# First MLP boundary: w2 products ahead of their row dots, one accumulator tile, last dots behind the norm

## The chip, the cores and the metric

One core of one Trainium2 chip runs the whole program in one launch. The metric is the device time of that core in microseconds (us), lower is better. The core has five engines that run side by side, each working through its own queue in order: PE (TensorE, matmuls and transposes), DVE (VectorE), ACT (ScalarE), POOL (GpSimd) and SP (SyncE, which here only issues DMA transfers). Sixteen DMA engines move data between HBM and the on-chip memory. An instruction waits in its queue until the semaphores that it names have been raised by the work that it depends on, and everything behind it in the same queue waits with it.

## What is computed

A decode step for one token through four layers, forward and backward: attention A, MLP B, attention A, MLP B, with the same weights and the same K and V caches in both attention layers. The loss gradient is given, and all gradients of inputs, weights and caches are outputs.

```python
def _A_ref(x, k_cache, v_cache, wq, wo):          # x: 1 x 1 x 1024, caches: 4 x 65536 x 128
    q = (x @ wq).reshape(B, Sq, Hq, Dh).transpose(0, 2, 1, 3)   # 32 heads of 128
    k = jnp.repeat(k_cache, rep, axis=1)
    v = jnp.repeat(v_cache, rep, axis=1)
    p = _softmax(einsum("bhqd,bhkd->bhqk", q, k) * Dh ** -0.5)
    o = einsum("bhqk,bhkd->bhqd", p, v)
    return o.transpose(0, 2, 1, 3).reshape(B, Sq, Hq * Dh) @ wo

def _B_ref(x, w1, b1, w2, b2):                    # w1: 1024 x 3584, w2: 3584 x 1024
    h = einsum("bsd,df->bsf", x, w1) + b1
    r = where(h > 0, h, 0)
    return einsum("bsf,fd->bsd", r * r, w2) + b2

x = A_x
x = x + _A_ref(_layernorm(x), ...)                # layer 1
x = x + _B_ref(_layernorm(x), ...)                # layer 2
x = x + _A_ref(_layernorm(x), ...)                # layer 3
x = x + _B_ref(_layernorm(x), ...)                # layer 4
```

## The kernel before

The kernel streams the caches through on-chip memory four times: attention layer 1, attention layer 3, the backward pass of layer 3, and the backward pass of layer 1, which also writes the gradients of both caches. Between them stand the MLP layers. The large gradients are written in the last pass.

**Memory.** The large on-chip areas are seven pairs (`pair0` to `pair12`) of two halves with 1 MB each, the tile `eT3`, whose four halves are used as areas until layer 3 needs them, and `small`, a tile of eight blocks of 128 x 1024 for transposed blocks and one broadcast vector. A `Ring` hands out the least recently used half (`slab`, L278: one transfer into one half) or pair (`Stream.fetch`, L301: one transfer of 2 MB). A transfer may start once whatever last used its area is done; SP issues transfers in order, so one that waits holds back those behind it.

**Products.** `mv_slab` (L405) multiplies one 128-row block of a weight matrix with a column of the activations: eight matmuls with a single column for 1024 columns of weights, accumulated into one PSUM tile over all blocks.

**Row dots.** The gradient of the hidden activations of layer 4 needs the product of every row of w2 with `grad_out`. Both are known as soon as w2 passes by, so the kernel does this work in layer 2, while w2 is on the chip: `RowDots.block` takes the 28 row blocks of w2 one by one and picks for each the cheapest of four ways by a running estimate of the load of DVE, ACT and PE:

- A: one fused multiply and sum on DVE (L463);
- B: a multiply on DVE (`dot_va`, L427), then a sum on ACT (L428);
- C: eight transposes on PE (L474) into a PSUM tile, a copy to `small` on DVE (L477), eight dots on PE (L482) into an accumulator tile of one column, and a copy of that column to `y` on DVE (L483);
- D: as C, with the copy on ACT (L479).

The multiplies of A and B write over the block in place, so they wait for the product that reads the same block.

**The first boundary.** After attention layer 1: the output projection (two slabs of Wo), the norm, eight slabs of w1, the hidden activations (`mlp_hidden`), then seven slabs of w2 with four row blocks each. For each row block the program has its product and then its row dot. `mlp_close` (L755, then L385) adds the bias and the residual; `new_layer` holds the norm of layer 3 (`ln_fwd`, L348 to L365); `q_first` loads two slabs of Wq and computes the query of the first head group; then `attn_fwd` begins. Its first 40 of 256 items (an item is eight blocks of 128 rows of K) need no load and no transposes, since layer 1 kept their transposed K in ten areas: they are scores only (L686), with a copy on ACT (L691) and a maximum on DVE (L692). In the meantime `q_rest` loads the remaining three groups' Wq in eight slabs of 768 KB and adds their products between the items; `q_at=(2, 3)` puts the first one at item 2 and each next one three items later. From item 40 on K is loaded in pairs (2 MB), transposed on PE (L667) and copied (L152 on ACT, L155 on DVE).

**Order.** The program is written once in one sequence, and the framework's scheduler then sets each engine's queue by its own estimates; the queues can differ from the order of the text. SP's order of transfers around this boundary is: seven w2 slabs, two Wq slabs for `q_first`, eight for `q_rest`, then K, and V when it is needed.

Past the first items of layer 3 the diff touches nothing; `dg4`, the result of the row dots, is first used in layer 4.

Of the kernel before, what the change touches and what calls it, by code (L numbers as in the profile page):

```python
# [11 lines left out]
ALU = mybir.AluOpType  # L12
AX = mybir.AxisListType
PSUM = bass.MemoryType.PSUM
P = 128
# [3 lines left out]
def kernel(  # L19
# [24 lines left out]
    nc = tc.nc  # L44
    NOSYNC = mybir.DependencyInfo(mybir.DependencyClass.NoSync, mybir.DependencyReason.DATA)
    D = A_x.shape[-1]
# [8 lines left out]
    DC, FC = D // P, F // P  # L55
    C = SK // P
# [32 lines left out]
    def ps_tr():  # L89
        return PS["pool"].tile([P, 8, P], BF, name="ps_tr", tag="tr", bufs=2 if PS["pass4"] else 3)  # L90
# [7 lines left out]
    def ps_acc(shape):  # L98
        return PS["pool"].tile(shape, F32, name="ps_acc", tag="acc", bufs=1)
# [17 lines left out]
    def ps_bg(shape, dtype=F32):  # L117
        return ps_small("bg", shape, dtype)
# [4 lines left out]
    ident_b = const.tile([P, P], BF, name="ident_b")  # L123
# [33 lines left out]
    def add_load(act=0.0, dve=0.0):  # L157
        load["act"] += act
        load["dve"] += dve
# [10 lines left out]
    for i in range(0, 14, 2):  # L170
        t = main.tile([P, 2 * SLOT], BF, name="pair%d" % i)
# [6 lines left out]
    small = main.tile([P, SMALL], BF, name="small")  # L178
# [4 lines left out]
    def part(ap, i, n):  # L183
        return ap[:, i * n:(i + 1) * n]
# [91 lines left out]
    def slab(src, a, n):  # L276
        v = ring.slot()[:, 0:a * n].rearrange("p (a n) -> p a n", n=n)
        nc.sync.dma_start(out=v, in_=src)  # L278
        return v
# [109 lines left out]
    def w_rows(W, r0, nk, c0, ncol):  # L389

        return W[r0:r0 + nk * P, c0:c0 + ncol].rearrange("(k p) n -> p k n", p=P)

    def slabs(W, r0, KC, c0, ncol):

        per = max(1, min(KC, SLOT // ncol))
        for k0 in range(0, KC, per):
            kn = min(per, KC - k0)
            v = slab(w_rows(W, r0 + k0 * P, kn, c0, ncol), kn, ncol)
            for kk in range(kn):
                yield k0 + kk, v[:, kk, :]  # L400

    def mv_slab(out, view, kc, KC, ncol, xcol):
        nb_ = ncol // P
        for nb in range(nb_):
            nc.tensor.matmul(out[:, nb:nb + 1], lhsT=view[:, nb * P:(nb + 1) * P], rhs=xcol,  # L405
                             start=(kc == 0 and nb == 0), stop=(kc == KC - 1 and nb == nb_ - 1), skip_group_check=True)
# [18 lines left out]
    def dot_va(view, vbc, ycol, n):  # L425

        nc.vector.tensor_tensor(out=view, in0=view, in1=vbc, op=ALU.mult)  # L427
        nc.scalar.activation(out=view, in_=view, func=ACTF.Copy, accum_out=ycol)  # L428
        add_load(act=0.39 + n * 0.00086, dve=0.14 + n * 0.00053)

    class RowDots:
# [14 lines left out]
        def block(self, kc, view):  # L446
            N, L = self.N, self.loads
            ncb = N // P
            ng = (ncb + 7) // 8
            np_ = self.pieces  # L450
            cpe = ncb * 0.17 + 0.1
            opts = {
                "A": (L["dve"] + 0.14 * np_ + N * 0.00107, L["act"], L["pe"]),
                "B": (L["dve"] + 0.14 * np_ + N * 0.00053, L["act"] + 0.39 * np_ + N * 0.00086, L["pe"]),
                "C": (L["dve"] + 0.15 * (ng + 1) + N * 0.00053, L["act"], L["pe"] + cpe),
                "D": (L["dve"] + 0.15, L["act"] + 0.19 * ng + N * 0.00081, L["pe"] + cpe),
            }
            best = min(opts, key=lambda k: (max(opts[k]), sum(opts[k])))
            L["dve"], L["act"], L["pe"] = opts[best]
            w = N // np_  # L460
            if best == "A":
                for p in range(np_):
                    nc.vector.scalar_tensor_tensor(out=view[:, p * w:(p + 1) * w], in0=view[:, p * w:(p + 1) * w], scalar=1.0, in1=self.vbc[:, p * w:(p + 1) * w],  # L463
                                                   op0=ALU.mult, op1=ALU.mult, accum_out=self.y[:, kc, p:p + 1])
            elif best == "B":
                for p in range(np_):
                    dot_va(view[:, p * w:(p + 1) * w], self.vbc[:, p * w:(p + 1) * w], self.y[:, kc, p:p + 1], w)
            else:
                py = ps_acc([P, 1])
                for g0 in range(0, ncb, 8):  # L470
                    gn = min(8, ncb - g0)
                    pt = ps_tr()
                    for i in range(gn):
                        nc.tensor.transpose(pt[:, i, :], view[:, (g0 + i) * P:(g0 + i + 1) * P], ident_b[:, :])  # L474
                    wt = WT.next()
                    if best == "C":
                        nc.vector.tensor_copy(out=wt[:, 0:gn, :], in_=pt[:, 0:gn, :])  # L477
                    else:
                        nc.scalar.copy(out=wt[:, 0:gn, :], in_=pt[:, 0:gn, :])  # L479
                    for i in range(gn):  # L480
                        cb = g0 + i
                        nc.tensor.matmul(py[:, :], lhsT=wt[:, i, :], rhs=self.vcb[:, cb:cb + 1], start=(cb == 0), stop=(cb == ncb - 1))  # L482
                nc.vector.tensor_copy(out=self.y[:, kc, 0:1], in_=py[:, :])  # L483

        def plan(self, steps, wt):

# [70 lines left out]
    def blocks(ap, i, n=1):  # L557

        return ap[:, i * 1024:(i + n) * 1024].rearrange("p (a b) -> p a b", b=P)
# [33 lines left out]
    def at(bg, i, fn):  # L593
        bg.setdefault(i, []).append(fn)

    def q_first(L, g):

        pq = ps_bg([P, R])
        for kc, view in slabs(A_wq, 0, DC, g * GD, GD):
            mv_slab(pq, view, kc, DC, GD, L["nb"][:, kc:kc + 1])  # L600
        set_q(L, pq, 0, [g])
# [544 lines left out]
    eT1, eT3 = Exps(1), Exps(3)  # L1146
    U, X1 = area[0:5], area[5:10]
    S0, S1 = pair[10], pair[12]
# [4 lines left out]
    ORD1, ORD2, ORD3, ORD4 = [0, 1, 2, 3], [3, 2, 1, 0], [0, 1, 2, 3], [3, 2, 1, 0]  # L1153
# [5 lines left out]
    kept1 = e3_halves + [area[10], area[11]]  # L1159
    ring.add(*e3_halves)  # L1160

    last = IPG * (G - 1)
# [10 lines left out]
    L2 = mlp_open(L1["xo"], "L2")  # L1173
# [3 lines left out]
    rd4 = RowDots(FC, D, gx[:], "B4_dg", vbc_small)  # L1177
    mlp_hidden(L2)
    pf = ps_bg([P, DC])
    for kc, view in slabs(B_w2, 0, FC, 0, D):  # L1180
        mv_slab(pf, view, kc, FC, D, L2["gb"][:, kc:kc + 1])
        rd4.block(kc, view)
    mlp_close(L2, pf[:, :])
    dg4 = rd4.result()
    L3 = new_layer(L2["xo"], "L3")
    q_first(L3, ORD2[0])
    ring.remove(area[12], area[13])


# [24 lines left out]
    def ahead_of_end(bg, ik):  # L1214
# [6 lines left out]
        for k, i in ((0, 4), (1, 7)):  # L1221
            at(bg, e - 12 + 4 * k, lambda k=k, i=i: wo_block(k, part(small, i, 1024), k == 0))
        at(bg, e - 6, lambda: (fetch_w1(area[12]), fetch_w1(area[13])))
    v_areas = attn_fwd(L3, ORD2, eT3, [S1, S0], more=ahead_of_end, have=kept1, q_at=(2, 3))
    v_kept = [v_areas[(ORD2[-1], b)] for b in range(NB - VKEEP, NB)]


# [87 lines left out]
    for kc in range(FC):  # L1315
        for i in range(DC):
            nc.tensor.matmul(pg2[:, kc:kc + 1], lhsT=w2T[kc][:, i, :], rhs=dx2b[:, i:i + 1],
                             start=(kc == 0 and i == 0), stop=(kc == FC - 1 and i == DC - 1), skip_group_check=True)
# [66 lines left out]
    done = [IPG * (j + 1) + LAG4 + 1 for j in range(G)]  # L1385
# [60 lines left out]
```

## Time and profile before

| | |
|---|---|
| time, median of 3 runs | 1994.94 us (1993.6 to 1997.81) |
| profiled execution, its own time | 1996.7 us |
| its span, first to last instruction | 1994.9 us |
| mean granted TensorE clock | 0.903 |
| busy share: PE, PEld, DVE, ACT, POOL | 80%, 66%, 55%, 51%, 10% |
| DMA | 793.86 MB, mean 398 GB/s |
| HBM read, written | 623.92 MB, 165.69 MB |

The page's second part cuts the span into 40 slices of about 49.9 us and gives for each the busy share of every engine in tenths, the clock that PE was granted, the busy share of the DMA engines and their rate. The first boundary lies in slices 8 and 9, counted from 1 (about 349 to 449 us). A row of the timeline is: start, duration, engine, line, operation, output and inputs by name, how many instructions were merged, and in brackets how long the engine had been idle before and what ended that. "issue" in a bracket is idle time for which the profile shows no releaser. SPq is the issue of a transfer on SP's queue. In a row of the waits the numbers are the total, the number of waits and the longest.

### The profile page before, as it was taken

How to read it: one execution, taken by the hardware profiler on the slowest of the kernel's cores; microseconds unless marked ns; L12 is line 12 of the kernel's file. 1: busy time of each engine (PE TensorE's matmuls, PEld its weight loads, DVE VectorE, ACT ScalarE, POOL GpSimd, SP SyncE). 2: the span in 40 equal slices, each digit the busy share in tenths (PEclk: the TensorE clock that was granted, in tenths of full speed). 3: DMA queues.
4: the chain of work that ended last, by engine and by line, in shares of the span. 5: the costliest groups of instructions: out<-in, count | busy, mean ns of one | idle time of the engine just before them, and what ended most of it. 6: DMA issues, size and time to landing. Idle time of an engine off the chain costs nothing.

```text
span 1994.9 us, 65729 instructions
## 1 busy us (share of the span) xinstructions
PE 1590.6 (80%) x29868; PEld 1316.1 (66%) x29924; DVE 1101.0 (55%) x1816; ACT 1026.5 (51%) x1284; POOL 204.4 (10%) x362
## 2 busy tenths in 40 slices
PE   7888886579888858888878876877888778788886
PEld 6878786578787757877777775555555545555464
DVE  4544431146444314645454456877677767787675
ACT  3543432034434314445444436876677667767775
POOL 0000000000000000000000001222122222212221
PEclk9998997669999976999889977999889978989898
DMA  9999999989999996999999996999999999999997
GB/s 395 426 423 421 411 408 410 406 317 419 425 421 420 425 409 275 397 418 412 412 412 396 403 390 240 412 425 424 387 418 408 423 406 367 423 372 420 423 422 302
DMA packets 119186, 793.86 MB, mean 398 GB/s; under 512 B 11756, under 2 KB 11770, under 8 KB 55290
## 3 DMA queue, kind: packets, MB, share of 16 engines
q1 hardware_dynamic: 82858, 604.02, 74.1%
q0 software_dynamic: 29136, 173.04, 21.0%
q10 hardware_dynamic: 6912, 12.59, 1.7%
q8 instruction: 234, 3.83, 0.8%
q14 instruction: 46, 0.38, 0.0%
HBM read 623.92 MB, written 165.69 MB: 396 GB/s over the span
## 4 chain that ended last, share of the span: by engine, by line
PE 38%; DMA 34%; DVE 10%; ACT 10%; issue 7%; another core or an unknown queue 0%; POOL 0%; SPq 0%; ACTq 0%; POOLq 0%; DVEq 0%
DMA pair<-in_A_v_cache_dram 15%; DMA pair<-in_A_k_cache_dram 8%; DMA out_dram<-pair 7%; PE ps_tr L667 6%; PE ps_sc L686 4%; PE ps_acc L729 4%; PE ps_gg L1082 4%; PE ps_tr L920 3%; PE ps_tr L1015 3%; ACT small L152 3%; ACT pair L152 3%; DVE pair L155 3%; DMA pair<-in_A_wo_dram 2%; DVE small L155 2%; PE ps_sc L941 2%
## 5 line engine op out<-in xcount | busy, mean ns | idle before, releaser
L155 DVE COPY small<-ps_tr 128x1024 bf16<-128x1024 bf16 x637 | 432.2, 688 | 338.1 <-PE ps_tr L667 172.8
L152 ACT COPY small<-ps_tr 128x1024 bf16<-128x1024 bf16 x371 | 372.8, 1015 | 387.6 <-PE ps_tr L667 206.8
L152 ACT CAST pair<-ps_gg 128x1024 bf16<-128x1024 f32 (+2 forms) x331 | 320.3, 983 | 141.1 <-PE ps_gg L1082 79.0
L155 DVE CAST pair<-ps_gg 128x1024 bf16<-128x1024 f32 x245 | 289.4, 1182 | 115.5 <-PE ps_gg L1082 91.3
L667 PE MATMUL ps_tr<-ident_b,pair 128*128 128x128 bf16 x3264 | 246.8, 225 | 29.2 <-DMA pair<-in_A_k_cache_dram 16.4
L1082 PE MATMUL ps_gg<-pair,small 64*128 64x512 bf16 x1024 | 201.5, 403 | 56.1 <-ACT pair L152 24.1
L667 PEld LDWEIGHTS <-pair 128*128 128x128 bf16 x3264 | 197.4, 101 | 34.8 <-DMA pair<-in_A_k_cache_dram 19.0
L729 PE MATMUL ps_acc<-eT,pair 128*128 128x64 bf16 x3840 | 170.4, 205 | 44.6 <-DMA pair<-in_A_v_cache_dram 39.8
L686 PE MATMUL ps_sc<-L_qpad,small 128*128 128x64 bf16 (+7 forms) x3456 | 173.9, 193 | 24.0 <-issue 10.7
L729 PEld LDWEIGHTS <-pair 128*128 128x128 bf16 x3840 | 154.0, 104 | 48.3 <-DMA pair<-in_A_v_cache_dram 42.9
L1015 PE MATMUL ps_tr<-ident_b,pair 128*128 128x128 bf16 x1792 | 163.4, 229 | 14.8 <-DMA pair<-in_A_v_cache_dram 11.6
L428 ACT ACTIVATE pair<-pair 128x1024 bf16<-128x1024 bf16 (+1 forms) x125 | 142.1, 1137 | 50.3 <-DVE pair L427 46.1
L920 PE MATMUL ps_tr<-ident_b,pair 128*128 128x128 bf16 x2048 | 155.6, 228 | 13.6 <-DMA pair<-in_A_v_cache_dram 9.8
L686 PEld LDWEIGHTS <-small 128*128 128x128 bf16 x3456 | 140.4, 99 | 34.6 <-ACT small L152 16.1
L1015 PEld LDWEIGHTS <-pair 128*128 128x128 bf16 x1792 | 115.7, 102 | 61.3 <-issue 42.8
L920 PEld LDWEIGHTS <-pair 128*128 128x128 bf16 x2048 | 128.6, 103 | 35.7 <-DMA pair<-in_A_v_cache_dram 17.8
L1082 PEld LDWEIGHTS <-small 64*128 64x128 bf16 x1024 | 60.5, 94 | 112.5 <-issue 85.0
L941 PE MATMUL ps_sc<-B_dOpad,small 128*128 128x64 bf16 (+7 forms) x2048 | 101.0, 193 | 16.0 <-ACT small L152 9.0
L1035 PE MATMUL ps_sc<-DOB,small 128*128 128x64 bf16 (+3 forms) x2048 | 112.1, 195 | 0.6 <-issue 0.2
L1035 PEld LDWEIGHTS <-small 128*128 128x128 bf16 x2048 | 87.0, 100 | 36.9 <-issue 32.0
L692 DVE TENSOR_REDUCE pm_all<-pair 128x8 f32<-128x512 f32 x64 | 43.9, 686 | 111.8 <-ACT pair L691 111.8
L941 PEld LDWEIGHTS <-small 128*128 128x128 bf16 x2048 | 80.1, 99 | 26.1 <-ACT small L152 14.1
(262 smaller groups left out, 1997.0 us busy)
## 6 DMA issues: line engine op xcount, KB each, us to landing
out_dram<-pair POOLq DMA_DIRECT2D x128, 1024.0 KB, 16.3
pair<-in_A_v_cache_dram SPq DMA_DIRECT2D x62, 2048.0 KB, 16.9
pair<-in_A_v_cache_dram SPq DMA_DIRECT2D x112, 1024.0 KB, 13.0
pair<-in_A_k_cache_dram SPq DMA_DIRECT2D x111, 1024.0 KB, 13.9
pair<-in_A_k_cache_dram SPq DMA_DIRECT2D x55, 2048.0 KB, 19.0
pair<-in_A_wo_dram SPq DMA_DIRECT2D x24, 1024.0 KB, 19.4
out_dram<-eT POOLq DMA_DIRECT2D x44, 512.0 KB, 16.5
pair<-in_B_w_dram SPq DMA_DIRECT2D x24, 896.0 KB, 15.1
```

The costliest lines, as they stand in the source:

```text
L152: nc.scalar.copy(out=out, in_=in_)
L155: nc.vector.tensor_copy(out=out, in_=in_)
L428: nc.scalar.activation(out=view, in_=view, func=ACTF.Copy, accum_out=ycol)
L667: nc.tensor.transpose(pt[:, i, :], kb8[:, i, :], ident_b[:, :])
L686: nc.tensor.matmul(ps_s[:, slot:slot + w, :].rearrange("p a b -> p (a b)"), lhsT=kt[:, i, :], rhs=L["qpad"][:, g, 0:w, :].rearrange("p a b ...
L692: nc.vector.tensor_reduce(out=pm_all[:, :, c0 // UB], in_=S_sb[:, :, c0:c0 + un], axis=AX.X, op=ALU.max)
L729: nc.tensor.matmul(ps_o[:, :, :].rearrange("p a b -> p (a b)"), lhsT=vb8[:, i, :], rhs=eT[g][:, :, c:c + 8], start=(c == 0), stop=(c == C ...
L920: nc.tensor.transpose(pt[:, i, :], vb8[:, i, :], ident_b[:, :])
L941: nc.tensor.matmul(ps_dp[:, slot:slot + w, :].rearrange("p a b -> p (a b)"), lhsT=vt[:, i, :], rhs=dOpad[:, g, 0:w, :].rearrange("p a b -> ...
L1015: nc.tensor.transpose(pt[:, i, :], vb8[:, i, :], ident_b[:, :])
L1035: nc.tensor.matmul(ps_dp[:, slot:slot + w, :].rearrange("p a b -> p (a b)"), lhsT=vt[:, i, :], rhs=DOB[:, g, 0:w, :].rearrange("p a b -> p ...
L1082: nc.tensor.matmul(pg[:, t2 * 512:(t2 + 1) * 512], lhsT=xt[64 * t2:64 * t2 + 64, blk0 + half, :], rhs=GG[64 * t2:64 * t2 + 64, :, :, :].re ...
```

## The change

A new method `RowDots.spread` replaces `block` for this one use. It returns two functions. `block` chooses among the same four ways with other prices, and its dots on PE go into one accumulator tile with a column for each of the 28 blocks; `done` copies the used columns to `y`. The transposed blocks go round five areas of `small` instead of two. The program now has the four products of a slab first and then the four row dots of that slab; the last slab's four dots stand behind `mlp_close`, the norm and `q_first`, followed by `done`. In layer 3 `q_at` becomes (1, 1): a Wq-rest product at each of items 1 to 8.

```diff
+        def spread(self, n, wt):
+            L = self.loads
+            py = ps_acc([P, n])
+            cols = []
+            def block(kc, view, last):
+                L["pe"] += 0.27
+                opts = {
+                    "A": (L["dve"] + 1.31, L["act"], L["pe"]),
+                    "B": (L["dve"] + 0.69, L["act"] + 1.25, L["pe"]),
+                    "C": (L["dve"] + 0.69, L["act"], L["pe"] + 1.2),
+                    "D": (L["dve"], L["act"] + 1.0, L["pe"] + 1.2),
+                }
...
+                else:
+                    pt = ps_tr()
+                    for i in range(8):
+                        nc.tensor.transpose(pt[:, i, :], part(view, i, P), ident_b[:, :])
+                    t = wt.next()
+                    (nc.vector.tensor_copy if best == "C" else nc.scalar.copy)(out=t, in_=pt[:, :, :])
+                    for i in range(8):
+                        nc.tensor.matmul(py[:, kc:kc + 1], lhsT=t[:, i, :], rhs=self.vcb[:, i:i + 1], start=(not cols and i == 0),
+                                         stop=(i == 7), skip_group_check=True)
+                    cols.append(kc)
+            def done():
+                for kc in cols:
+                    nc.vector.tensor_copy(out=self.y[:, kc, 0:1], in_=py[:, kc:kc + 1])
+            return block, done
...
     pf = ps_bg([P, DC])
-    for kc, view in slabs(B_w2, 0, FC, 0, D):
-        mv_slab(pf, view, kc, FC, D, L2["gb"][:, kc:kc + 1])
-        rd4.block(kc, view)
+    rd_block, rd_done = rd4.spread(FC, Turn([blocks(small, i) for i in (5, 6, 0, 1, 2)]))
+    w2_here = list(slabs(B_w2, 0, FC, 0, D))
+    for k0 in range(0, FC, 4):
+        for kc, view in w2_here[k0:k0 + 4]:
+            mv_slab(pf, view, kc, FC, D, L2["gb"][:, kc:kc + 1])
+        if k0 + 4 < FC:
+            for kc, view in w2_here[k0:k0 + 4]:
+                rd_block(kc, view, False)
     mlp_close(L2, pf[:, :])
-    dg4 = rd4.result()
     L3 = new_layer(L2["xo"], "L3")
     q_first(L3, ORD2[0])
+    for kc, view in w2_here[FC - 4:]:
+        rd_block(kc, view, kc == FC - 1)
+    rd_done()
+    dg4 = rd4.result()
...
-    v_areas = attn_fwd(L3, ORD2, eT3, [S1, S0], more=ahead_of_end, have=kept1, q_at=(2, 3))
+    v_areas = attn_fwd(L3, ORD2, eT3, [S1, S0], more=ahead_of_end, have=kept1, q_at=(1, 1))
```

## The prediction

> **What bounds the kernel now.** I read the page first, its second part above all. The DMA engines are busy nearly everywhere, so the time is the bytes plus the places where DMA has nothing to do. One such place is slice 9 (slices of 49.9 us: 399 to 449 us), 317 GB/s where its neighbours have 406 and 419:
>
> ```profile
> PEclk9998997669999976999889977999889978989898
> DMA  9999999989999996999999996999999999999997
> GB/s 395 426 423 421 411 408 410 406 317 419 425 421 420 425 409 275 397 418 412 412 412 396 403 390 240 412 425 424 387 418 408 423 406 367 423 372 420 423 422 302
> ```
>
> That is the first boundary, so I asked for its stretches: w2 streaming, its tail, the norm, the scores on kept K, the stream after (columns: stretch, its length, busy us of PE, PEld, DVE, ACT, POOL, clock, DMA share, GB/s).
>
> ```profile
> 391.00:405.00 14.00, 10.75 (x217) 10.48 (x218) 9.16 (x18) 8.50 (x13) 0.00 (x0) 0.50 1.05 386
> 405.00:418.30 13.30, 10.12 (x210) 9.69 (x207) 9.04 (x23) 7.99 (x13) 0.00 (x0) 0.50 0.94 356
> 418.30:424.70 6.40, 3.44 (x78) 3.15 (x79) 2.27 (x15) 0.85 (x3) 0.00 (x0) 0.50 0.53 193
> 424.70:443.50 18.80, 15.91 (x512) 15.68 (x512) 3.44 (x5) 2.93 (x5) 0.00 (x0) 0.86 0.74 276
> 443.50:480.00 36.50, 33.12 (x694) 31.98 (x691) 27.18 (x51) 14.05 (x27) 0.61 (x4) 0.92 1.01 427
> ```
>
> Against the shares of the full stretches (1.05 and 1.01) DMA loses 13.3 x 0.11/1.05 = 1.4, 6.4 x 0.48/1.01 = 3.0 and 18.8 x 0.27/1.01 = 5.0 us: 9.4 us, the most that this place can give. Then the DMA queue's own waits there, 385 to 445 us (total, times, longest), which say who holds the slots:
>
> ```profile
> SPq L278 <- PE ps_bg L405: 12.6, 4, 3.9
> SPq L278 <- ACT pair L428: 10.1, 5, 4.3
> SPq L301 <- PE ps_bg L405: 9.7, 2, 6.6
> ```
>
> Row dots (ACT L428) hold the Wq slabs; Wq products (PE ps_bg L405) hold the last Wq slabs and the first K transfers (L301). The timeline gives the order:
>
> ```profile
> 391.65 0.59 PE L405 MATMUL ps_bg<-L_gb,pair 128*128 128x1 bf16 x16 [1.79 <-DMA pair<-in_B_w_dram]
> ...
> 394.43 0.69 DVE L477 COPY small<-ps_tr 128x1024 bf16<-128x1024 bf16 x1 [0.40 <-PE ps_tr L474]
> ...
> 395.24 0.35 PE L482 MATMUL ps_acc<-rd_vcb,small 128*128 128x1 bf16 x8 [0.65 <-DVE B_dg L483]
> ...
> 418.30 0.15 DVE L755 TENSOR_TENSOR ffn_f<-ps_bg,b2c 128x8 f32<-128x8 f32 x1
> ...
> 422.33 1.85 PE L405 MATMUL ps_bg<-L_nb,pair 128*128 128x1 bf16 x64 [1.11 <-DVE L_nb L365]
> ...
> 434.25 0.74 PE L405 MATMUL ps_bg<-L_nb,pair 128*128 128x1 bf16 x24
> ...
> 435.02 0.33 SPq L301 DMA_DIRECT2D pair<-in_A_k_cache_dram  x1
> 435.40 0.42 SPq L301 DMA_DIRECT2D eT<-in_A_k_cache_dram  x1
> ...
> 442.67 0.35 PE L405 MATMUL ps_bg<-L_nb,pair 128*128 128x1 bf16 x8 [2.62 <-issue]
> ```
>
> The seven w2 slabs land every 2.69 us, 391.6 to 407.8, but blocks end only at 418.3 (26.6 us, 3.8 per slab of four). The norm takes 4.0 us to 422.3. The first new K transfer goes out at 435.02, behind the fourth Wq-rest product (434.25 + 0.74); from its landing (443.4) DMA is full again. So the path is: last w2 product, norm, first Wq product, four Wq-rest products among the scores, K issue. What that issue moves, the end moves, since DMA is full behind it.
>
> **Part 1: products ahead of dots.** PE's queue in the changed kernel reads, for each slab: 32 products, the transposes of its one or two PE blocks, their dots, then the next slab. The balance gives PE 10 blocks instead of 13 (slabs 0 to 5: one, two, one, two, one, two), ACT sums 13 instead of 10, DVE fused multiplies 5 as before. A slab's period on PE, from rows of this stretch at 0.50 clock: 32 products 0.95, eight transposes 1.01 (the next eight start after 0.80), copy 0.69 on DVE (L477) or 1.01 on ACT (L479), eight dots 0.20 until the next may start, 0.05 for each handover. One block: 0.95 + 1.01 + 0.05 + 0.69 + 0.05 + 0.20 = 2.95, with an ACT copy 3.27. Two blocks: 0.95 + 0.80 + 1.01 + 0.05 + 0.69 + 0.05 + 0.20 = 3.75, with ACT copies about 4.15. The six: 2.95 + 4.15 + 3.27 + 3.75 + 2.95 + 3.75 = 20.8 us. From 391.65 that is 412.5; with 1.1 for the last slab's products the close (ffn_f) starts at 413.6. The period's bounds: 2.69 (slabs can't come faster) and about 5.0 (every copy stands behind a 1.23 us multiply). I take 3.5, near the sum, because DVE has 5 x 1.28 + 19 x 0.62 = 18.2 us and ACT 13 x 1.20 + 4 x 0.91 = 19.2 us to do in 22 us: both have slack, so copies wait little. With 0.2 for that: 413.8, 4.5 us earlier. The shared accumulator tile takes away PE's wait for the y copies (L483; 2.2 us in sum in this stretch), which the periods above already leave out.
>
> **Part 2: last dots behind the norm.** Not quite: DVE's queue puts the fused multiply of block 25 (1.28) between ffn_f and the sum to xo, the product of block 27 (0.62) before ln_s, and ten y copies between the norm's small steps, five of them before ln_ss. PE has the last eight transposes and dots between the norm's two sums, ACT the last sum ahead of the root; these run beside DVE. Price: 1.28 + 0.62 less 0.44, what lay between xo and ln_s before, plus five copies that cost 0.07 to 0.16 each when their operands are ready. That is 1.8 to 2.3; the copies partly fill waits of 0.4 to 0.7 us for PE's sums, so 1.6. The bounds are 0.5 and 3.0. The norm then takes 5.6 us and the first Wq products start at 413.8 + 5.6 = 419.4, 2.9 us earlier. Their second slab landed at 413.07, so it is there.
>
> **Part 3: Wq products one per item, q_at (2, 3) to (1, 1).** PE's queue shows each Wq-rest product at its old place among the scores; only slots change. The last Wq slab takes the other half of pair 6, so it waits for the second Wq-rest product, not for a kept area; its issue was 427.87 and becomes about 427.5: nothing. The second K transfer loses its slot in the eT tile and goes to pair 0, behind the fifth and sixth Wq-rest products (436.6 to 439.5 before, so about 436.5 after). The first K transfer needs 4.9 us of DMA from about 433.1, to 438; the second, issued at 436.5 to 437, needs 1.25 us to its first packet. It just fits: cost 0 to 0.3, and up to 2.7 if PE's sequencer stalls there as it did at 440 (2.62, the row above).
>
> **Part 4: clock.** The scores start cold: 0.50 until 428.6 after a whole busy window (425.20 to 428.60: PE busy 3.40), then 1.00. Starting at 421.8 they can fill the window from 421.8 to 425.2, which gains 0.3 us; if they just miss it, the cold stretch is longer by one step of 3.4 us, a loss of about 1.1 us at the fourth product. I take the gain. The Trainium skill, "TensorE: Matmul & The Clock Gate", Part 1, says the activity window is 3413 ns and free-running, and that the transition depends on where in it the work begins. The steps of this trace agree; by that rule the sum would be anything between these two ends from run to run.
>
> **Elsewhere.** All later queues are nearly the same; slots are renamed, the distance between two uses of a slot differs by one transfer here and there. One wait is new: in the backward pass the Wq slab for area 6, issued at 897.24, will wait for dots on a Wo slab that end near 908.5. Transfers already queued keep every DMA engine busy until 916.5 (first landing of the one before it), 8 us of cover; were it gone, up to 11 us of SP's queue would show. Cost 0.
>
> **Sum:** -4.5 + 1.6 - 0.3 = -3.2 us at the first K issue. The profiled execution took 1996.7 (span 1994.9 and 1.8 around it), 1.8 above the median of the three runs; its time would be 1993.5, and the median 1994.94 becomes 1991.7.
>
> **Rivals.** (a) The whole hole closes: were the slabs paced by DMA alone and the norm no longer than before, ffn_f would start at 409 and the Wq products at 413.1, where their slab lands: 9.2 us earlier; less about 1.5 for the K issue behind PE: 1987.2. For it: DVE and ACT need 2.75 us per slab, about DMA's 2.69. Against: PE's queue, where dots stand before the next products. (b) Slower: exactly that order lets a late copy hold the next slab's products. From a mean period of 4.0 us the Wq products start no earlier than before; each 0.1 above costs 0.6. At the upper bound, 5.0, it is +6; I price it at 4.8, +5: 1999.9. For it: copies already wait behind multiplies (idle PE of 2.7 us for L477). Against: the slack above. (c) Nothing: the 2.6 us stall falls before the sixth Wq-rest product, and the second K transfer, which no longer has its own slot, leaves DMA idle for most of what was won: about -0.5, 1994.4.
>
> **Chances.** The forecast case 0.55, with its own spread of -1.5 to -6; (a) 0.20; (b) 0.12; (c) 0.13. About 0.2% (4 us) is what a measurement of this kernel can tell from no change. Of the forecast case 0.25 lies beyond that (period 3.3 or the norm at its lower bound are enough), so faster 0.45, same 0.43, slower 0.12. The range reaches down to most of (a) and up to half of (b): 1986.5 to 1998.
>
> **What would show it.** Right: ffn_f near 413.8 and the first Wq products near 419.4 (times shifted with the w2 landing); PE waiting for copies, not for DMA, between slabs; K's first issue near 431.8; the DMA share of the stretch from the norm to kept K's end up from 0.69, with about 6 us lost instead of 9.4. Wrong: a slab period above 4.0; a norm above 7 us; a hole in DMA between the first and second K transfers; or a loss at the second or third boundary (slices 16 and 25, 275 and 240 GB/s), which the sum holds unchanged.

## The result, and the profile after

The changed kernel takes 1991.75 us (median of 17 runs, 1985.22 to 1994.22), the kernel before, run beside it, 1994.94 (17 runs, 1991.12 to 1998.02). The ratio, which is one of means, is 0.998 with a 95% interval of 0.9973 to 0.9987: 4.0 us faster (2.6 to 5.4), where the medians lie 3.2 us apart. The profiled execution took 1990.63 us (span 1988.9).

First the slices of the page, as in the prediction. Slice 9 rises from 317 to 337 GB/s: the hole at the first boundary got smaller but did not close. The second and third boundaries, slices 16 and 25, have 268 and 240 GB/s (before 275 and 240).

```profile
PEclk9999998669999977999889977999989988999898
DMA  9999999989999996999999996999999999999997
GB/s 394 425 425 420 415 407 409 407 337 425 423 421 421 425 407 268 405 419 411 411 413 396 410 376 240 413 424 424 408 415 402 424 400 373 422 389 421 423 421 296
```

Then the stretches of the boundary, cut at the changed kernel's own marks (stretch, length, busy us of PE, PEld, DVE, ACT, POOL, clock, DMA share, GB/s):

```profile
391.30:405.00 13.70, 10.56 (x216) 9.40 (x216) 10.53 (x17) 9.41 (x15) 0.00 (x0) 0.50 1.05 386
405.00:413.05 8.05, 6.69 (x155) 6.08 (x156) 5.89 (x9) 5.42 (x10) 0.00 (x0) 0.50 1.04 398
413.05:420.80 7.75, 4.08 (x85) 3.61 (x84) 4.25 (x27) 3.35 (x6) 0.00 (x0) 0.50 0.83 320
420.80:437.40 16.60, 16.55 (x512) 16.46 (x511) 3.34 (x5) 2.93 (x5) 0.60 (x4) 0.80 0.70 258
437.40:480.00 42.60, 36.78 (x784) 35.42 (x785) 30.57 (x58) 15.57 (x28) 0.00 (x0) 0.92 1.01 419
```

DMA is full through the w2 tail (1.04, where it was 0.94) and busier in the norm (0.83, where it was 0.53). What is lost is 0.1 us in the tail, 7.75 x 0.22/1.05 = 1.6 in the norm and 16.6 x 0.31/1.01 = 5.1 in the scores, in all 6.8 us instead of 9.4. The largest part of the hole is now the stretch of scores on kept K, where PE has no idle time (16.55 of 16.60 us). The DMA queue's own waits, 385 to 445 us (total, times, longest), say who holds the slots. The row dots' ACT sums hold them for 6.9 us instead of 10.1, their transposes on PE for 7.0 instead of 6.0, and the Wq products still hold the K transfers for 9.0 (before 9.7).

```profile
SPq L278 <- PE ps_bg L405: 9.7, 3, 4.4
SPq L301 <- PE ps_bg L405: 9.0, 3, 4.2
SPq L278 <- PE ps_tr L511: 7.0, 4, 3.0
SPq L278 <- ACT pair L428: 6.9, 5, 2.5
```

The timeline gives the order (start, us, engine, line). From the first product of one slab to that of the next it takes 2.90, 4.12, 3.21, 3.74, 2.96 and 3.80 us.

```profile
391.29 1.01 PE L405 MATMUL ps_bg<-L_gb,pair 128*128 128x1 bf16 x32 [1.76 <-DMA pair<-in_B_w_dram]
...
394.19 0.99 PE L405 MATMUL ps_bg<-L_gb,pair 128*128 128x1 bf16 x32
...
398.31 0.99 PE L405 MATMUL ps_bg<-L_gb,pair 128*128 128x1 bf16 x32
...
412.02 0.99 PE L405 MATMUL ps_bg<-L_gb,pair 128*128 128x1 bf16 x32
...
413.05 0.17 DVE L794 TENSOR_TENSOR ffn_f<-ps_bg,b2c 128x8 f32<-128x8 f32 x1
413.14 1.22 DVE L504 SCALAR_TENSOR_TENSOR pair<-pair,small 128x1024 bf16<-128x1024 bf16 x1
...
418.46 1.85 PE L405 MATMUL ps_bg<-L_nb,pair 128*128 128x1 bf16 x64 [1.11 <-DVE L_nb L365]
...
431.69 6.65 SPq L301 DMA_DIRECT2D pair<-in_A_k_cache_dram  x4
...
440.47 1.78 PE L706 MATMUL ps_tr<-ident_b,pair 128*128 128x128 bf16 x15 [3.12 <-DMA pair<-in_A_k_cache_dram]
```

The marks of this boundary in every profile, in us after w2's first product on PE (391.0 to 391.7): ffn_f (the last w2 product is done), the first Wq product, the first new K transfer issued, the first transposes of new K on PE, and the sum of PE's "issue" stalls between the Wq products and those transposes or among the first of them (up to 447 us). "Wo" is the landing of one later slab, the fourth Wo slab of layer 3's K and V pass (646.51 in the profile before), as a shift against before, taken from the same w2 product. The last columns are the median time and the ratio to the kernel before, on the same chip, with its interval. The experiments ran on several chips, on which the kernel before had medians of 1994.09 to 1995.51 us, so the text compares ratios.

| kernel | ffn_f | Wq | K issue | new K on PE | stalls | Wo | us | ratio |
|---|---|---|---|---|---|---|---|---|
| before | 26.65 | 30.68 | 43.38 | 51.88 | 2.88 | 0 | 1994.94 | 1 |
| after | 21.77 | 27.18 | 40.40 | 49.19 | 0 | -2.74 | 1991.75 | 0.9980 (0.9973 to 0.9987) |
| e1 old Wq places | 21.77 | 27.17 | 41.60 | 50.55 | 1.21 | -2.16 | 1994.32 | 0.9993 (0.9983 to 1.0003) |
| e2 last dots before norm | 23.48 | 27.60 | 40.53 | 49.30 | 0 | -2.45 | 1990.83 | 0.9982 (0.9973 to 0.9990) |
| e3 block by block | 21.02 | 26.34 | 39.34 | 48.06 | 0 | -3.75 | 1990.58 | 0.9982 (0.9972 to 0.9991) |
| e4 no row dots | 17.23 | 21.11 | 34.42 | 45.24 | 3.77 | -5.25 | 1988.35 | 0.9970 (0.9957 to 0.9983) |
| e5 early K | 21.77 | 27.18 | 33.59 | 50.46 | 3.86 | -2.34 | 1992.61 | 0.9996 (0.9987 to 1.0005) |
| e6 before, early K | 26.64 | 30.68 | 37.09 | 50.83 | 2.86 | -0.99 | 1993.07 | 0.9995 (0.9987 to 1.0004) |
| e7 block by block, early K | 21.04 | 26.36 | 32.77 | 49.65 | 3.99 | -3.06 | 1990.55 | 0.9983 (0.9973 to 0.9993) |
| e8 own accumulators | 21.85 | 27.24 | 40.25 | 49.35 | 0 | -2.98 | 1991.17 | 0.9977 (0.9967 to 0.9987) |
| e9 before, new ways | 23.14 | 26.95 | 42.08 | 51.22 | 2.44 | -1.76 | 1991.68 | 0.9985 (0.9976 to 0.9994) |
| e10 after, old ways | 23.39 | 28.59 | 42.01 | 51.35 | 3.82 | -1.14 | 1993.62 | 0.9989 (0.9980 to 0.9997) |
| e11 before, q_at (1, 1) | 26.64 | 30.67 | 44.07 | 53.27 | 3.54 | +1.50 | 1996.64 | 1.0004 (0.9995 to 1.0013) |
| e12 new ways and places | 23.14 | 27.14 | 39.33 | 48.18 | 0 | -3.89 | 1990.27 | 0.9979 (0.9970 to 0.9987) |

### The profile page after: what moved, and what is told of

Read it like the earlier page. It is cut to its first block, busy times and chain, and to the rows that moved or that the text cites. A ratio compares the mean times of both kernels' runs of the same rounds, so it can differ in the third digit from the quotient of the medians.

```text
span 1988.9 us, 65697 instructions
## 1 busy us (share of the span) xinstructions
PE 1589.4 (80%) x29876; PEld 1306.1 (66%) x29876; DVE 1101.9 (55%) x1816; ACT 1026.4 (52%) x1287; POOL 203.4 (10%) x362
## 3 DMA queue, kind: packets, MB, share of 16 engines
q8 instruction: 233, 3.82, 0.8%
## 4 chain that ended last, share of the span: by engine, by line
DMA 38%; PE 34%; DVE 11%; ACT 10%; issue 5%; POOL 0%; SPq 0%; ACTq 0%; DVEq 0%; POOLq 0%
DMA pair<-in_A_v_cache_dram 16%; DMA pair<-in_A_k_cache_dram 9%; DMA out_dram<-pair 8%; PE ps_tr L706 5%; PE ps_sc L725 3%; PE ps_tr L959 3%; ACT pair L152 3%; PE ps_gg L1121 3%; PE ps_acc L768 3%; ACT small L152 3%; PE ps_tr L1054 3%; DVE pair L155 2%; DVE small L155 2%; PE ps_gg L1172 2%; DMA pair<-in_A_wo_dram 2%
## 5 line engine op out<-in xcount | busy, mean ns | idle before, releaser
L155 DVE COPY small<-ps_tr 128x1024 bf16<-128x1024 bf16 x639 | 433.6, 687 | 343.0 <-PE ps_tr L706 180.5
L725 PEld LDWEIGHTS <-small 128*128 128x128 bf16 x3456 | 138.4, 99 | 27.8 <-ACT small L152 17.2
L1074 PEld LDWEIGHTS <-small 128*128 128x128 bf16 x2048 | 87.1, 100 | 37.3 <-issue 32.8
L1172 PE MATMUL ps_gg<-pair 128*128 128x512 bf16 x240 | 81.4, 422 | 25.8 <-DVE pair L155 12.4
## 6 DMA issues: line engine op xcount, KB each, us to landing
pair<-in_A_k_cache_dram SPq DMA_DIRECT2D x111, 1024.0 KB, 13.5
```

Source lines behind the costliest of these rows:

```text
L155: nc.vector.tensor_copy(out=out, in_=in_)
L725: nc.tensor.matmul(ps_s[:, slot:slot + w, :].rearrange("p a b -> p (a b)"), lhsT=kt[:, i, :], rhs=L["qpad"][:, g, 0:w, :].rearrange("p a b ...
L1074: nc.tensor.matmul(ps_dp[:, slot:slot + w, :].rearrange("p a b -> p (a b)"), lhsT=vt[:, i, :], rhs=DOB[:, g, 0:w, :].rearrange("p a b -> p ...
L1172: nc.tensor.matmul(pg[:, q0:q0 + qq], lhsT=av[:, kb + kk, :], rhs=b_rows[:, n0 + m0 + q0:n0 + m0 + q0 + qq], start=True, stop=True)
```

## Experiments

The diffs are against the changed kernel, those of e6, e9, e11 and e12 against the kernel before.

**e1: the Wq products at their old places.**

```diff
-    v_areas = attn_fwd(L3, ORD2, eT3, [S1, S0], more=ahead_of_end, have=kept1, q_at=(1, 1))
+    v_areas = attn_fwd(L3, ORD2, eT3, [S1, S0], more=ahead_of_end, have=kept1, q_at=(2, 3))
```

> The changed kernel with q_at back at (2, 3). My theory: the places of the Wq products among the items change slots only. The last Wq slab and the second K transfer go back to the eT tile, but the first K transfer still waits for the fourth Wq-rest product: K's first issue 40.4 us after w2's first product (within 0.7 us), as in the changed kernel, and the time within 2 us of its 1991.75. Rival: the new Wq places are what frees DMA earlier; then K's first issue is 2 us or more later than 40.4 and the time goes back toward 1995.

Up to the first Wq product nothing differs. Then PE stops for 1.21 us just before the fourth Wq-rest product, and the first K issue comes 1.2 us later. The timeline of e1:

```profile
423.89 0.90 SPq L278 DMA_DIRECT2D eT<-in_A_wq_dram  x1
...
431.86 0.30 PE L725 MATMUL ps_sc<-L_qpad,pair 128*128 128x64 bf16 x5 [1.21 <-issue]
...
432.78 0.33 SPq L301 DMA_DIRECT2D pair<-in_A_k_cache_dram  x1
```

"Issue" means that PE waited for nothing that the profile shows. The trace has a 16 KB packet of PE's instruction queue (q8 on the page) at 429.64 to 430.61; in the changed kernel the packet at this point of the program ran from 427.45 to 428.65. In e1 the last Wq slab went out without a wait at 423.89 and was moving then; in the changed kernel it goes out only at 427.11. So in these traces the new places are worth 1.2 us at the K issue, though not in the way that the prediction gave; that lies between what I expected (0.7 us at most) and the rival (2 us or more). By the ratios e1 takes 2.6 us more than the changed kernel, but the intervals overlap.

**e2: the last slab's dots ahead of the norm, as before.**

```diff
-        if k0 + 4 < FC:
-            for kc, view in w2_here[k0:k0 + 4]:
-                rd_block(kc, view, False)
+        for kc, view in w2_here[k0:k0 + 4]:
+            rd_block(kc, view, kc == FC - 1)
+    rd_done()
     mlp_close(L2, pf[:, :])
```

> The changed kernel with the last slab's four dots ahead of mlp_close again. My theory: deferring trades one delay for another. The close comes about 1.8 us later (23.6 us after w2's first product instead of 21.8), the norm is shorter by about 1.2 (4.4 instead of 5.4), so the first Wq products start 0.6 us later and the time is 1992.3, within 1.5 us of the changed kernel. Rival: the deferral is the main part of the gain; then the first Wq products start 2 us or more later than in the changed kernel (over 29.2 us after w2's first product).

ffn_f comes 1.71 us later and the norm takes 4.1 us instead of 5.4, so the first Wq product is 0.4 us later and the K issue 0.1. Putting the last dots behind the norm only moves their cost from one side of ffn_f to the other, and the times agree (0.9982 and 0.9980).

**e3: product and dot block by block.** The order of the kernel before inside a slab, everything else as changed (the last slab's dots still behind the norm).

```diff
     for k0 in range(0, FC, 4):
         for kc, view in w2_here[k0:k0 + 4]:
             mv_slab(pf, view, kc, FC, D, L2["gb"][:, kc:kc + 1])
-        if k0 + 4 < FC:
-            for kc, view in w2_here[k0:k0 + 4]:
+            if k0 + 4 < FC:
                 rd_block(kc, view, False)
```

> The changed kernel with product and row dot of each block in turn again, the last slab's dots still behind the norm, the new prices and the one accumulator tile kept. My theory after the result: PE's queue was limited by waits for copies, which a product between transposes and dots can fill, so taking all products of a slab first is not what gained: the close comes 0.9 us EARLIER (20.9 us after w2's first product), K's first issue at 39.5, the time about 1991. Rival, the change's own words: products ahead of the dots free PE's path; then the close is 2 us or more later than 21.8.

ffn_f comes 0.75 us earlier than in the changed kernel. Products ahead of their dots, the first thing the change names, is not what gained; with the new prices it costs a little. In the time the two can't be told apart.

**e8: an accumulator tile for each block,** with its copy to y at once.

```diff
+                    py = ps_acc([P, 1])
...
-                        nc.tensor.matmul(py[:, kc:kc + 1], lhsT=t[:, i, :], rhs=self.vcb[:, i:i + 1], start=(not cols and i == 0),
-                                         stop=(i == 7), skip_group_check=True)
+                        nc.tensor.matmul(py[:, :], lhsT=t[:, i, :], rhs=self.vcb[:, i:i + 1], start=(i == 0), stop=(i == 7))
+                    nc.vector.tensor_copy(out=self.y[:, kc, 0:1], in_=py[:, :])
```

> The changed kernel with an accumulator tile of one column for every PE block again (one buffer, so that each block's dots wait for the copy of the last one's column). My theory: with dots batched behind a slab's products only the second block of a pair can wait, and by then DVE has copied: the close comes within 0.4 us of 21.8 us after w2's first product, the norm is 0.3 us shorter because no column copies are left in it, the time equals the changed kernel's within 1.5 us. Rival: the wait for the column copies (2.2 us in the profile of before) was the gain; then the close is 1.5 us or more later.

ffn_f comes 0.08 us later, and the norm takes 5.40 us, as in the changed kernel (5.41): in this order neither the common tile nor the column copies matter. That the ten copies lengthen the norm, as I expected, is wrong. They stand where DVE would wait anyway: without them its wait for the root (L360) is 0.97 us instead of 0.65.

**e4: the floor.** This kernel leaves out the row dots of w2 in layer 2, so the gradients that need them are not computed; it shows what the place could give if the dots cost nothing.

```diff
-    rd_block, rd_done = rd4.spread(FC, Turn([blocks(small, i) for i in (5, 6, 0, 1, 2)]))
...
-                rd_block(kc, view, False)
...
-    rd_done()
```

> The changed kernel without the row dots of w2 in layer 2 (the gradient of layer 4's hidden activations is left at zero): what the place could give if the dots cost nothing, rival (a) of the prediction. My theory: the close comes with the last slab, 17.2 us after w2's first product instead of 21.8, the norm takes 4.0 instead of 5.4, the first Wq products start at 21.2 to 21.8 (their second slab lands then), K's first issue 35 to 36.5 instead of 40.4, and the time is 4 to 5.5 us below the changed kernel's: 1987. Rival: the remaining hole in DMA is set by the slots and not by this path; then the time stays within 1.5 us of the changed kernel's.

The waits of e4's PE, 395 to 446 us (total, times, longest):

```profile
PE ps_bg L405 <- DMA pair<-in_B_w_dram: 8.4, 5, 1.7
PE ps_sc L725 <- issue: 3.8, 2, 2.5
PE ps_tr L706 <- DMA pair<-in_A_k_cache_dram: 2.1, 1, 2.1
```

Now DMA paces the slabs, ffn_f is at 17.23 and the Wq products at 21.11. But 9.57 us at the Wq products become 6.6 at the first transposes and 5.25 at the Wo slab. On the way PE loses 3.77 us to two stalls (before 2.88), ahead of the fifth and the sixth Wq-rest product. The second K transfer waits for the sixth product and goes out only at 435.15, 9.7 us behind the first, and from 430.5 to 435.2 DMA has a share of 0.37: that is the hole which rival (c) of the prediction described, here without the dots. Against the kernel before, the change and the missing dots together are worth 6.0 us (3.4 to 8.6), of which the change has 4.0. That leaves 2.0 us between e4 and the changed kernel, where I had expected 4 to 5.5.

**e5, e6, e7: the first K blocks into kept areas.** If the K issue sets the end, it need not wait for the Wq products: two pairs of K blocks go to areas whose K the scores have finished, at items 9 and 17, and the last two Wq products move to items 10 and 11.

```diff
+        def into(self, g, b, w, halves):
+            v = w.rearrange("p (j d) -> p j d", d=DH)
+            nc.sync.dma_start(out=v, in_=self.views[g][b // 2])
...
+        for i, b, w, halves in early:
+            at(bg, i, lambda b=b, w=w, halves=halves: kstream.into(order[0], b, w, halves))
...
-    v_areas = attn_fwd(L3, ORD2, eT3, [S1, S0], more=ahead_of_end, have=kept1, q_at=(1, 1))
+    v_areas = attn_fwd(L3, ORD2, eT3, [S1, S0], more=ahead_of_end, have=kept1, q_at=(1, 1, (10, 11)), early=[(9, 10, wides[-2][0], e3_halves[0:2]), (17, 12, wides[-1][0], e3_halves[2:4])])
```

e5 is the changed kernel with this, e6 the kernel before with this, e7 is e3 with this.

> The changed kernel, with the first two K transfers sent early into the two pairs of eT whose kept blocks the scores have done with (items 9 and 17), and the last two Wq slabs at items 10 and 11 behind the first of them. In the changed kernel PE waits 3.1 us for the first K transfer (437.35 to 440.47), whose slot waits for the fourth Wq-rest product. My theory: that slot is now the bound, so K's first issue comes at 33 to 35 us after w2's first product instead of 40.4, PE does not wait for it, and the time falls by 3 to 4 us to 1988. Rival: PE is the bound from here on (transposes of 0.68 us an item, 5.4 us for each transfer of 4.9), so an earlier K is given back and the time stays within 1 us.

> The kernel before, with the same early K transfers as e5 and nothing of the change. My theory: the row dots, norm and first Wq product stay where they were (26.6, 4.0 us), K's first issue goes from 43.4 us after w2's first product to 36.5 to 38.5, but PE reaches the first transposes only at 51, near where it was (51.9); DMA gains about 3 us: 1991.5, as much as the change under study. Rival: there PE is the bound and the time stays within 1 us of 1994.6.

> Both: block by block as in e3 (close at 21.0, 0.75 us earlier than in the changed kernel) and the early K transfers of e5. My theory: gains add where both lie on the path of DMA: 3.5 to 4.5 us below the changed kernel, 1987.5, and not slower than e5. Rival: once K is early the norm no longer decides, and e7 equals e5 within 0.5 us in the trace (first K landing and the stream behind it).

All three missed. In e5 the K issue is 6.8 us earlier than in the changed kernel and the first K lands at 433.6 instead of 440.4; DMA's share from 420.80 to 437.40 is 0.85 instead of 0.70. And the time is no better (by the ratios 3.2 us worse, with intervals that touch). In the changed kernel no transfer of this pass goes to the eT tile, so e5 takes no area away from the stream. Two things are seen. PE's timeline in e5 has two stalls, so that PE is at the new K 1.3 us later than in the changed kernel, although that K is there:

```profile
432.85 0.31 PE L734 MATMUL ps_sc<-L_qpad,pair 128*128 128x64 bf16 x5 [2.05 <-issue]
...
439.59 1.66 PE L734 MATMUL ps_sc<-L_qpad,pair 128*128 128x64 bf16 x35 [1.81 <-issue]
```

And the stretches 470 to 480 and 480 to 490 show that DMA gives back what it was ahead. First the changed kernel's two, then e5's:

```profile
470.00:480.00 10.00, 8.21 (x187) 7.50 (x185) 5.02 (x10) 7.45 (x14) 0.00 (x0) 1.00 1.00 423
480.00:490.00 10.00, 9.48 (x229) 9.18 (x228) 4.63 (x8) 4.43 (x6) 0.00 (x0) 1.00 1.01 426
470.00:480.00 10.00, 8.36 (x182) 8.05 (x180) 5.33 (x10) 8.82 (x21) 0.00 (x0) 0.88 0.96 359
480.00:490.00 10.00, 9.75 (x230) 9.40 (x228) 4.83 (x7) 4.20 (x5) 0.00 (x0) 0.95 0.94 344
```

The queue's waits, 443 to 520 us, name what it waits for: PE's transposes of the K that is already there, in e5 (second row) once for 13.5 us, in the changed kernel (first row) for 6.9 at most.

```profile
SPq L301 <- PE ps_tr L706: 50.3, 10, 6.9
SPq L301 <- PE ps_tr L715: 51.4, 8, 13.5
```

So here DMA got ahead of PE only as far as the slots held. How much of the loss is the stalls' and how much the slots' was not tried apart.

**e9, e10, e11, e12: the ways of the dots.** With the new ways, order, tile and last dots had each come out at next to nothing. What was left is that the new function also chooses anew which engine does which dot: 10 blocks over PE instead of 13, 13 sums on ACT instead of 10. e9 is the kernel before with the new list of ways, e10 the changed kernel with the old list, e11 the kernel before with q_at (1, 1) alone, e12 the kernel before with the new ways, q_at (1, 1) and the five copy buffers.

```diff
 e9:
-        rd4.block(kc, view)
+        rd4.block(kc, view, "BCBADABDABDABCBCBBCBCBBCBADB")
 e10:
-                best = min(opts, key=lambda k: (max(opts[k]), sum(opts[k])))
-                if last and not cols:
-                    best = "C"
+                best = "ADBCBCBDABCBDADADBCBCBCBDABC"[kc]
 e12, beside the edits of e9 and e11:
+    wt2, WT = WT, Turn([blocks(small, i) for i in (5, 6, 0, 1, 2)])
```

> The kernel before with one thing changed: each of the 28 row dots of this loop takes the way that the changed kernel gives it (10 blocks over TensorE instead of 13, 13 sums on ScalarE instead of 10). Order, accumulator tiles, two buffers for the copies, last dots ahead of the norm and q_at stay as before. Theory (the ways are the gain): ffn_f 22.7 to 23.5 us after w2's first product instead of 26.65, the norm 4.0, the first Wq product at about 27 instead of 30.68; the first K issue at about 41.5, since the old places of the Wq products cost 1.2 in the run with these alone; time about 1993.5. Rival (the order, or the five buffers for the copies, is the gain): ffn_f at about 26 and the time at the kernel before's.

> The changed kernel with the ways of the kernel before (13 blocks over TensorE, 10 sums on ScalarE), everything else as changed. Theory (the ways are the gain): three more blocks of about 1 to 1.5 us on TensorE's path, ffn_f 24.5 to 26 us after w2's first product instead of 21.8, the norm 5.4, the first Wq product at 30 to 31; time 1994.5, no better than the kernel before. Rival (the order, the buffers or the accumulator are the gain): ffn_f at 22 and 1991.5.

> The kernel before with q_at (1, 1) alone. The local milestones up to the first Wq product stay as before (26.65, 30.7). Theory (the Wq products' places decide only whether TensorE stalls for its instructions there and where the second K block goes): within 1.5 us of the kernel before, and slower by about 1 us if the stall of 2.6 us stays ahead of the sixth product, which now holds the second K transfer. Rival (the places are worth what the changed kernel lost without them, 2.5 us): 1992.4.

> The kernel before with the new ways, five buffers for the copies and q_at (1, 1): all that is left out of the change is the order (products of a slab ahead of its dots), the common accumulator tile and the last dots behind the norm. Theory: ffn_f at about 22.7 us after w2's first product, the norm 4.0, the first Wq product at 26.7, the first K issue at 39.8; time 1990.7, as good as the changed kernel or 1 us better. Rival (the parts left out carry some of the gain): ffn_f above 24 and 1993 or more. Against the kernel with the new ways alone, a later or earlier ffn_f tells what the three extra buffers do.

The ways alone (e9) bring ffn_f 3.51 us forward and the first Wq product to 26.95, where the whole change has it (27.18). The timeline of e9:

```profile
414.18 0.16 DVE L757 TENSOR_TENSOR ffn_f<-ps_bg,b2c 128x8 f32<-128x8 f32 x1
...
418.00 1.85 PE L405 MATMUL ps_bg<-L_nb,pair 128*128 128x1 bf16 x64 [1.11 <-DVE L_nb L365]
...
432.05 0.43 PE L688 MATMUL ps_sc<-L_qpad,pair 128*128 128x64 bf16 x5 [2.44 <-issue]
...
433.12 0.33 SPq L301 DMA_DIRECT2D pair<-in_A_k_cache_dram  x1
```

Behind it, e9 loses 2.44 us to a stall as e1 did, so at the K issue 1.3 of the 3.7 us are left. With q_at (1, 1) as well (e12) the stall is gone, and the kernel is as fast as the changed one. e12's ffn_f is e9's, so the three extra copy buffers do nothing there. e11 shows q_at by itself: no gain. A stall of 0.90 us ahead of the fourth Wq-rest product (before 0.26) makes the first K issue 0.7 us later. The second K transfer, which before went out at 435.40, now waits for the sixth product and goes out at 440.31. The long stall stands in the seventh product, as it did before the change, and new K starts 1.39 us later:

```profile
439.54 0.74 PE L405 MATMUL ps_bg<-L_nb,pair 128*128 128x1 bf16 x24
...
440.26 0.54 PE L405 MATMUL ps_bg<-L_nb,pair 128*128 128x1 bf16 x16
443.15 1.00 PE L405 MATMUL ps_bg<-L_nb,pair 128*128 128x1 bf16 x32 [2.35 <-issue]
```

e10 came out between theory and rival: the old ways cost 1.6 us at ffn_f and 1.4 at the Wq products, not about 3; with them the rest of the change still brings ffn_f 3.3 us and the Wq products 2.1 us forward against before. So the two do not add up: at the Wq products the ways alone give 3.7, all but the ways 2.1, both 3.5. In the time they give 3.0 us (1.2 to 4.8), 2.2 (0.6 to 4.0) and 4.0 (2.6 to 5.4). The new ways are enough, then, but they are not the only way to most of the gain. Which parts of that 2.1 are the order's, the moved last dots' or the buffers' was not run with the old ways.

Of the kernels with all the dots e8 (0.9977) and e12 (0.9979) have the lowest ratios, next to the changed kernel (0.9980), e2, e3 (0.9982 both) and e7 (0.9983). All six beat the kernel before, and their intervals overlap. e12 has its 0.2% without the new order, the common tile and the moved dots.

## Why the prediction was right, and where it was not

**Part 1, the slab period:** right to 0.1 us as a sum, but it does not tell the cause. The six periods were to be 2.95, 4.15, 3.27, 3.75, 2.95 and 3.75, 20.8 in all; measured 20.7. Nothing had to be added for waits, so ffn_f was at 413.05, not 413.8, 4.9 us earlier after w2's first product instead of 4.5. But the title "products ahead of dots" gave the credit to the order, and the sentence on the accumulator tile gave it 2.2 us of PE's waits. e3 shows that with the new ways the order costs 0.75, e8 that the tile is worth 0.1, e9 that 3.5 come with the ways by themselves. With the old ways all the rest together brings 3.3 at ffn_f (e10), of which the norm, longer by about 1.2, takes back a part. The sum could not show any of this, since it priced the finished queue, in which all of them are mixed.

**Part 2, the norm:** 5.4 us instead of the 5.6 given, +1.4 for +1.6. The fused multiply stands behind ffn_f as foreseen (413.14, 1.22 us). The share put on the y copies was nothing (e8).

**Part 3, the Wq places:** the second K transfer went out at 436.11 (given about 436.5) and landed at 445.33, 4.9 us behind the first: cost 0, as forecast. The 1.25 us from issue to first packet are too many: the traces have 0.95 for the first K transfer, before (435.02 to 435.98) and after (431.69 to 432.64). That the new places also spare a stall of 1.2 us (e1) to 2.4 us (e9 against e12) was not seen; the stall was thought of only as a risk of the change.

**Part 4, the clock:** it fell on the other side. PE's scores began at 420.80 at half clock, the stretch from 420.6 to 424.0 holds 3.20 of 3.40 us of PE work, and full clock came only at 427.4, after the next one, which is all work (3.40). It is so in all fourteen profiles: of the two stretches of 3.41 us ahead of full clock the last is all work, and the one before it, which did not bring full clock, holds 2.1 to 3.2 us. The first Wq product to the K issue then took 13.22 us instead of 12.70, +0.5 for the -0.3 given. e12 had the same start (420.71) and full clock from about 424.4, and needs 12.19 for the same way. This agrees with the rule of the Trainium skill, "TensorE: Matmul & The Clock Gate", Part 1, that the window runs freely: from the first score to full clock the profiles have 3.7 to 6.6 us. The page gives a spread of 500 ns either way; the 2.9 us between these ends are more.

**The sum:** -4.9 + 1.4 + 0.5 = -3.0 at the K issue, for -3.2; with the start of w2 0.36 earlier it came at 431.69 (given 431.8). About 6 us of lost DMA were foreseen, 6.8 found. That the median then agrees to 0.1 us is luck, when the interval is 2.8 us wide. The spans of the two profiled executions differ by 6.0 us, more than the boundary gave; what goes beyond comes late: the output writes near 1370 us start 2.7 us earlier than before, the last ones 6.1. There profiles differ from run to run (e12, earlier at this boundary than the changed kernel, has a span of 1992.2).

**The step that failed is "what that issue moves, the end moves".** It held for the change, where PE came forward with the issue. e5, e6 and e7 issue K 6.3 to 10.6 us before the kernel before does and gain 0.8, 1.0 and 3.4 us (e7 has no more than e3 has without it). Over the twelve experiments and the changed kernel the ratio goes with the start of new K on PE (correlation 0.87) and hardly with the K issue (0.27). That difference rests on e5 to e7: without these three the K issue has 0.86. The shift of new K on PE lies in the interval of the time for ten of the thirteen and misses it by at most 0.5 us (e9); the shift of the K issue lies in it for nine and misses it by 0.4 us in e4 and by 3.7 to 7.2 in e5 to e7. The better term was PE's arrival at new K: the landing when nothing stalls, PE's own stalls when K is early. How the shift is handed on from there is less clear. The Wo column agrees with the times (correlation 0.87, all thirteen in their intervals), but it is one slab of eight. The first Wo slab of that pass, which lands at 557.04 before, has 0.84, and six of the thirteen lie outside.

**Elsewhere:** the new wait for area 6 is there. That Wq slab is issued at 905.84 (before 897.24; given 908.5), and DMA has shares of 1.00 and 1.01 from 895 to 905 and from 905 to 916: no cost.

**The rivals:** (a) is e4, 1988.35 with the dots gone, so the price of 1987.2 was near, but no arrangement that does the dots came to it. (b)'s mechanism, a copy that holds the next products, fits the 0.75 us that the order costs at ffn_f (e3), not 5. (c) did not happen in the changed kernel; e4 shows its mechanism, a stall ahead of the sixth Wq-rest product that holds the second K transfer and leaves DMA at a share of 0.37. In e11 the long stall comes one product later, and its time, +0.8 us (-1.0 to +2.6), shows neither gain nor loss.

## What to carry to other kernels

A rewrite that changes an order and, on the way, the prices of a balance is two changes: run each alone. Here the balance alone gave 3.0 us, the rest alone 2.2 and both 4.0, so a part that is worth nothing on top of the other is not worth nothing by itself. An earlier transfer need not bring an earlier end: 6.3 us at the K issue brought 1.0 us in e6 (-0.8 to 2.6, against the kernel before), and 6.8 us brought none in e5 (against the changed kernel). So follow the consumer's first use and not the issue alone. When a stretch is moved, look at the sequencer's stalls again; in these kernels they sum to anything from 0 to 3.99 us.

## What had not been expected of the hardware

PE's "issue" stalls stand next to 16 KB packets of its instruction queue. Between 424 and 447 us there are fifteen longer than 0.7 us in eight of the kernels tried and the kernel before (0.77 to 3.05 us), and each ends 1.2 to 1.6 us after such a packet ends. Some of them, with both times in us:

| kernel | packet ends | PE goes on |
|---|---|---|
| before | 441.27 | 442.67 |
| e1 | 430.61 | 431.86 |
| e5 | 431.36, 438.14 | 432.85, 439.59 |
| e9 | 430.67 | 432.05 |
| e10 | 429.98, 440.17 | 431.33, 441.54 |

In the kernels without a stall the packet of this place ended at 427.6 to 429.0, and PE did not stop. The page of the changed kernel counts 233 of them, for 59752 instructions of PE and PEld, about 256 each:

```profile
q8 instruction: 233, 3.82, 0.8%
```

The Trainium skill, "Runtime: NRT & Kernel Launch", Instruction fetch mechanics, says that instructions come in 16 KiB blocks and that the crossing is mostly hidden. The size agrees; the fifteen stalls were not hidden. That the packet comes late because data stand ahead of it fits e1 against the changed kernel (2.2 us later while the Wq slab moves), but it was not tried by itself.
